# Weight-conversion pieces given fixed places among the expert slots, and the experts' first relu moved to ScalarE and ahead of the w2 splits

## The chip, the cores and the metric

The kernel runs on one core of a Trainium2 chip. A core has five engines with a queue each: PE (TensorE, matmuls), DVE (VectorE), ACT (ScalarE), POOL (GpSimd) and SP (SyncE, which here only issues DMAs). Every engine works through its own queue in the order of the program and waits for the others through semaphores. The metric is the device time of one execution, in microseconds.

## The reference, cut to what matters

```python
def _moe_ref(x, w_gate, w_output_gate, w1, w2):        # x: 1792 x 768, 8 experts, w1: 768 x 1024, w2: 1024 x 768
    e_idx = np.argmax(x @ w_gate, axis=1)
    ...
    for e in range(E):
        mask = e_idx == e
        h = np.maximum(x[mask] @ w1[e], 0.0)
        out[mask] = gate_w[mask, None] * eom[mask, e, None] * (h @ w2[e])

def _moe2_ref(x, w_in, w_out):                         # w_in: 768 x 2048, w_out: 2048 x 768
    h = x @ w_in
    return (h * np.cos(h)) @ w_out

x = sigmoid_attention(q, k, v)                         # 4 x 12 heads, 448 x 64, gives x
return _moe2_ref(_moe_ref(x, ...), w_in, w_out)
```

## The kernel before, in words

The program has three stages: attention, the experts (a mixture-of-experts layer with one expert for each token), and a second dense layer. All large matmuls are done three times, on a high and a low part of both operands, so that every operand is first split: ACT writes the high part (a Copy), DVE subtracts it to get the low part.

**Experts.** Tokens are sorted by expert into slots of 128, each slot with one expert. `slot(s, ...)` does one slot. For the measured data 19 slots, 0 to 18, are active, and new experts begin in slots 4, 6, 10, 11, 14, 15 and 18 (and 0). In a slot PE does, in this order: x times the first half of w1 (six k steps of three matmuls, tile `ph`, named `p` in the trace), three k steps of the second half, four transposes of the first half's relu (`turn_h`, tile `pht`), the other three k steps, six transposes of the next slot's tokens (`turn`, tile `pxt`), the first k step of h times w2 (tile `py`), four transposes of the second half's relu, and the other seven k steps with w2. The relu of each half (`relu`, tiles `hr`) reads PSUM; `turn_h` then has ACT write `hh` and DVE write `hl`.

The weights of an expert come in four quarters of w1 and four of w2, all through the same four buffers `rw`. In the slot before a new expert `split1` splits w1's quarters (`w1h` on ACT, `w1l` on DVE) and then has SP load w2's quarter into the same buffer. In the expert's first slot `split2(i)` splits w2's quarter i (`w2h`, `w2l`) and has SP load a quarter of the w1 that comes after. In other slots both are skipped by a branch on a flag. Before the change, `split2(0)` stands behind the first relu, `split2(1)` behind `turn_h` of the first half, and `split2(2)` and `split2(3)` ahead of `turn_h` of the second half. At the slot's end `scale_y` scales the result (`ysb`).

**Conversion.** The second layer's weights are given in float64, and the chip converts them itself in 48 pieces of 512 columns (`conv`). A piece is, in its first half, ACT's `cta`, POOL's maximum, ACT's `ctu` and DVE's `ctb` and `ctu`; and in its second half four DVE operations (`cta`, `chi`, `ctb`, `clo`). `conv_step()` finishes a piece that is open (`conv_end`), has SP store a finished piece (`conv_store`) and load the raw data of the next one (`conv_load`, two buffers `craw`), and begins a piece; unless told `False` it also finishes it. The attention does 23 pieces, the ends of slots 1 to 17 do one each (`CONV_EARLY = 40`), and the second layer does the other eight, one in each of its units 1 to 8, begun with `conv_step(False)` and finished within the next unit's `product`.

**Second layer.** `units` are pairs of a block of tokens (four blocks of 4, 4, 3 and 3 tiles) and one of 16 chunks of 128 columns. In unit u the program emits: `load_w(u + 5)`, `product(u + 1)` (with `conv_end` inside it, tiles `r`, `gh`, `gl`), `up(u + 2)` on PE, `take(u + 2)` on ACT (tile `p`, which empties PSUM), `angle(u + 2)` on DVE, then from unit 8 to 13 a transpose of the next block's tokens (`turn_y`, tiles `pyt` and `yl`), a conversion piece, `cosine(u + 2)` on ACT and `down(u)` on PE. `up` and `turn_y` share two PSUM buffers in turn. `load_w(c)` may not load a chunk that isn't converted:

```python
ready = max(i for i, (which, h, _) in enumerate(conv_list) if h == (c * P // CW if which == "i" else c // 2))
while conv_at[0] <= ready:
    conv_step()
```

For chunk 12, loaded in unit 7, `ready` is 44; for chunk 14, loaded in unit 9, it is 47.

Of the kernel before, what the change touches and what calls it, by code (L numbers as in the profile page):

```python
# [9 lines left out]
F32 = mybir.dt.float32  # L10
# [12 lines left out]

GATE_STEPS = 7
NEST = 18
CONV_EARLY = 40
PAUSE = "pause"
NRING = 6
ROUTE_AT = [(0, "relu"), (0, 9), (0, 15), (0, 17), (1, 0), (1, 3), (1, "relu"), (1, 9), (1, 14)]
# [25 lines left out]
def tile_attn_moe_cos(ctx: ExitStack, tc: tile.TileContext, q, k, v, wg, wog, w1, w2, w_in, w_out, out):  # L55
# [139 lines left out]
    def conv_end():  # L195
        while conv_rest:
            next(conv_rest.pop(), None)
# [31 lines left out]
            in_offset=bass.IndirectOffsetOnAxis(ap=at, axis=0),  # L229
        )  # L230

    def turn(xg, ps, tag):
        for k0, n_ in ((0, 4), (4, 2)):
            pt = ps.tile([P, 512], F32, tag=tag, name="pxt")
            for kc in range(n_):
                nc.tensor.transpose(pt[:, kc * P : (kc + 1) * P], xg[:, (k0 + kc) * P : (k0 + kc + 1) * P], ident)
            ptv = pt[:, : n_ * P].rearrange("p (k t) -> p k t", t=P)
            nc.scalar.activation(xh[:, k0 : k0 + n_], ptv, AF.Copy)  # L238
            nc.vector.tensor_tensor(
                xl[:, k0 : k0 + n_], ptv, xh[:, k0 : k0 + n_].bitcast(F32), op=ALU.subtract  # L240
            )

    def mm1(ps, nh, kc, first, last):
        i = 2 * nh + kc // 3
# [440 lines left out]
    with ExitStack() as st:  # L685
# [12 lines left out]
        def relu(ps, scalar=False):  # L698
            hr = m2.tile([P, 512], F32, tag="hr", name="hr")
            if scalar:  # L700
                nc.scalar.activation(hr, ps, AF.Relu)
            else:
                nc.vector.tensor_scalar(hr, ps, 0.0, None, op0=ALU.max)
            return hr
# [35 lines left out]
        def slot(s, between, when):  # L740
            nxt = s + 1 < NSLOT
            ahead = min(s, 1)
            hh = m2.tile([P, KF, P], F32R, tag="hh", name="hh", bufs=1)
            hl = m2.tile([P, KF, P], F32R, tag="hl", name="hl", bufs=1)
            with when():
                if 0 < s < NSLOT - 2:
                    gather(xgs[s % 2], idx[:, s + 2 : s + 3])
                if s > 1:
                    new = flag(1, s, SPLIT)
                    ld = flag(3, s, [ENG.SP])  # L750
                    ne = flag(0, s, [ENG.SP], E - 1)

                def split2(i):
                    if s == 0:
                        split(w2r[i], w2h[i], w2l[i])
                    elif s > 1:
                        with tc.If(new != 0):
                            split(w2r[i], w2h[i], w2l[i])
                        with tc.If(ld != 0):
                            nc.sync.dma_start(w1r[i], w1_src_d(ne, i))  # L760

                ph = p0 if s == 0 else ps_h.tile([P, 512], F32, tag="h", name="p0")
                for kc in range(3 if s == 0 else 0, KD):
                    mm1(ph, 0, kc, kc == 0, kc == KD - 1)
                    between(kc)
                hr0 = relu(ph, s == 0)
                between("relu")
                split2(0)
                p1 = ps_h.tile([P, 512], F32, tag="h", name="p1")
                for kc in range(KD):  # L770
                    mm1(p1, 1, kc, kc == 0, kc == KD - 1)
                    if kc == 2:
                        turn_h(hr0, hh, hl, 0)
                        split2(1)
                    between(KD + kc)
                hr1 = relu(p1, s <= 1)
                if 0 < s and nxt:
                    turn(xgs[(s + 1) % 2], ps_t, "t")
                if s > 0:
                    split2(2)  # L780
                    split2(3)
                py = ps_y.tile([P, 2, 512], F32, tag="y", name="py")
                state["py"] = py
                for kc in range(ahead):
                    mm2(py, hh, hl, kc)
                    between(2 * KD + kc)
                turn_h(hr1, hh, hl, 1)
                between("h")
                if s == 0:
                    split2(2)  # L790
                    split2(3)
            if nxt and s >= NSURE:
                split1(s + 1)
            with when():
                for kc in range(ahead, KF):
                    mm2(py, hh, hl, kc)
                    between(2 * KD + kc)
                if s == 0:
                    turn(xgs[1], ps_t, "t")
                elif nxt and s < NSURE:  # L800
                    split1(s + 1)
                if s > 0:
                    scale_y(s)
            if s >= 1 and conv_at[0] < CONV_EARLY:
                conv_step()

        def scale_y(s):
# [208 lines left out]
        split_first(3)  # L1016

        def last_slots(s):
            assert conv_at[0] >= CONV_EARLY
            act = nc.values_load(fl[0:1, 2, s : s + 1], min_val=0, max_val=1)  # L1020
            with tc.If(act != 0):
                slot(s, between(s), nullcontext)
                store_y(s)
                if s + 1 < NSLOT:
                    last_slots(s + 1)
# [254 lines left out]
```

## Time and profile before

| what | value |
|---|---|
| time, median of 3 runs | 1086.42 us (1086.36 to 1087.2) |
| the profiled execution: its time | 1089.18 us |
| the profiled execution: its span | 1087.5 us |
| PE busy | 1038.9 us, 96% of the span |
| DVE busy | 705.1 us, 65% |
| ACT busy | 486.6 us, 45% |
| POOL busy | 168.5 us, 15% |
| mean granted TensorE clock | 0.987 |

The times in the views are from the start of the span, which is shorter than the execution's own time by what lies before the first and after the last instruction. A line such as L703 is a line of the kernel; a wait in square brackets is idle time just before an instruction, and the name behind the arrow is what ended it.

### The profile page before, as it was taken

To read this page: it belongs to the slowest core of one execution; us is meant where nothing else is said; L and a number is where in the kernel's file an instruction comes from. 1 tells how busy PE (TensorE), PEld (TensorE's weight loads), DVE (VectorE), ACT (ScalarE), POOL (GpSimd) and SP (SyncE) were. 2 spreads that over 40 slices of the span, in tenths; PEclk is the share of its full clock that TensorE was granted. 3 is DMA by queue.
4 is the path that set the end of the run, shared out by engine and by line. 5 is a ranking of instruction groups with operands and counts; after the bars stand their busy time and mean duration, and the time that the engine had idled before them with its cause. 6 is when DMAs were issued, how large, how long until landed. Compare 5 with 4: busy or idle time off the path is not lost. (4 is left out here: it accounts for less than half of the span.)

```text
span 1087.5 us, 16874 instructions
## 1 busy us (share of the span) xinstructions
PE 1038.9 (96%) x5836; PEld 832.1 (77%) x5836; DVE 705.1 (65%) x1233; ACT 486.6 (45%) x707; POOL 168.5 (15%) x184
## 2 busy tenths in 40 slices
PE   6999999989999998998997999999999999999997
PEld 3555555568877886886786888788888899999996
DVE  3777778785767458658656599855555555665553
ACT  5777776532445245345334444333333343334332
POOL 3433332011111111211111032003000020001001
PEclk9999999999999999999899999999999999999999
DMA  7899995835578439939835998757644577668741
GB/s 186 250 283 299 261 260 169 306 101 184 182 255 312 125 123 348 322 121 352 269 113 181 392 359 304 259 184 255 244 174 179 184 297 298 247 232 286 261 165 44
DMA packets 118788, 254.68 MB, mean 234 GB/s; under 512 B 9440, under 2 KB 66016, under 8 KB 118688
## 3 DMA queue, kind: packets, MB, share of 16 engines
q1 hardware_dynamic: 114768, 234.19, 63.9%
q0 software_dynamic: 3920, 19.28, 4.6%
q8 instruction: 48, 0.79, 0.3%
q14 instruction: 52, 0.43, 0.1%
HBM read 207.02 MB, written 46.41 MB: 233 GB/s over the span
## 5 line engine op out<-in xcount | busy, mean ns | idle before, releaser
L1172 PE MATMUL o<-wo,gh 128*128 128x512 f32 x448 | 168.4, 397 | 0.0
L155 POOL TENSOR_SCALAR cta<-cta 128x512 f32<-128x512 f32 x48 | 77.3, 1610 | 458.6 <-ACT cta L154 458.6
L1112 PE MATMUL ph<-yh,wi 128*128 128x512 f32 (+1 forms) x318 | 115.3, 363 | 0.0
L1113 PE MATMUL ph<-yl,wi 128*128 128x512 f32 (+1 forms) x318 | 115.2, 362 | 0.0
L1114 PE MATMUL ph<-yh,wi 128*128 128x512 f32 (+1 forms) x318 | 115.2, 362 | 0.0
L1135 ACT ACTIVATE r<-r 128x512 f32<-128x512 f32 (+1 forms) x64 | 37.0, 578 | 168.6 <-DVE r L1130 167.0
L305 ACT ACTIVATE aT<-sc,b_sig 112x896 f32<-112x896 f32 x96 | 91.5, 1005 | 43.2 <-PE sc L302 42.3
L1173 PE MATMUL or<-wo,gh 128*128 128x256 f32 x384 | 108.5, 282 | 0.0
L1172 PEld LDWEIGHTS o<-wo,gh 128*128 128x128 f32 x448 | 84.1, 188 | 17.0
L246 PE MATMUL p<-w1h,xh 128*128 128x512 f32 x228 | 93.3, 409 | 0.3 <-ACT xh L238 0.3
L247 PE MATMUL p<-w1l,xh 128*128 128x512 f32 x228 | 90.7, 398 | 0.0
L248 PE MATMUL p<-w1h,xl 128*128 128x512 f32 x228 | 90.3, 396 | 0.0
L1172 PE MATMUL o<-wo,gl 128*128 128x512 f32 x224 | 88.3, 394 | 0.0
L309 PE MATMUL av<-aT,v 112*64 112x448 f32 x384 | 84.0, 560 | 1.4 <-DVE xT L319 1.4
L1141 DVE TENSOR_TENSOR r<-r,p 128x512 f32<-128x512 f32 (+1 forms) x64 | 40.0, 625 | 66.4 <-ACT r L1136 66.4
L1173 PEld LDWEIGHTS or<-wo,gh 128*128 128x128 f32 x384 | 72.4, 189 | 0.8
L1196 POOL DMA_INDIRECT out_dram<-osb,at x14 | 14.2, 1014 | 368.3 <-DVE osb L1185 277.0
L1126 DVE TENSOR_SCALAR t<-p 128x512 f32<-128x512 f32 (+1 forms) x64 | 27.1, 424 | 66.1 <-ACT p L1121 66.1
L1121 ACT ACTIVATE p<-ph 128x512 f32<-128x512 f32 (+1 forms) x64 | 34.7, 542 | 71.5 <-PE ph L1114 71.5
L1146 DVE TENSOR_TENSOR gl<-r,gh 128x512 fp32r<-128x512 f32 (+1 forms) x64 | 42.5, 664 | 36.4 <-ACT gh L1145 36.4
L1112 PEld LDWEIGHTS ph<-yh,wi 128*128 128x128 f32 x318 | 59.7, 188 | 7.7
L712 ACT ACTIVATE hh<-pht 128x512 fp32r<-128x512 f32 x38 | 22.7, 598 | 94.0 <-PE pht L709 84.2
(255 smaller groups left out, 2438.7 us busy)
## 6 DMA issues: line engine op xcount, KB each, us to landing
rw<-in_moe_w_dram SPq DMA_DIRECT2D x64, 768.0 KB, 6.1
wo<-wo_d SPq DMA_DIRECT2D x64, 768.0 KB, 4.4
wi<-wi_d SPq DMA_DIRECT2D x53, 768.0 KB, 5.9
craw<-in_moe_w_in_dram SPq DMA_DIRECT2D x25, 512.0 KB, 6.4
craw<-in_moe_w_out_dram SPq DMA_DIRECT2D x24, 512.0 KB, 5.5
er<-wi_d SPq DMA_DIRECT2D x11, 768.0 KB, 6.3
ys_d<-ysb SPq DMA_DIRECT2D x19, 384.5 KB, 3.7
wi_d<-chi SPq DMA_DIRECT2D x24, 256.0 KB, 3.1
```

Source lines behind the costliest of these rows:

```text
L155: nc.gpsimd.tensor_scalar(ta.bitcast(F32), ta.bitcast(F32), LEAST, None, op0=ALU.max)
L246: nc.tensor.matmul(ps, xh[:, kc], wh, start=first, stop=False)
L247: nc.tensor.matmul(ps, xh[:, kc], wl, start=False, stop=False)
L248: nc.tensor.matmul(ps, xl[:, kc], wh, start=False, stop=last)
L305: nc.scalar.activation(aT[:, c], ps[:, :, :S], AF.Sigmoid, bias=b_sig[:CP], scale=1.0 / math.sqrt(D))
L309: nc.tensor.matmul(pav[D * j : D * j + D, :S], t["v"][:, j, c, :], aT[:, c, j], start=c == 0, stop=c == NC - 1)
L1112: nc.tensor.matmul(ph[:, :w], wih[:, kc], yh[:, kc, :w], start=kc == 0, stop=False)
L1113: nc.tensor.matmul(ph[:, :w], wih[:, kc], yl[:, kc, :w], start=False, stop=False)
L1114: nc.tensor.matmul(ph[:, :w], wil[:, kc], yh[:, kc, :w], start=False, stop=kc == KD - 1)
L1146: nc.vector.tensor_tensor(gl[:, :w], r, gh[:, :w].bitcast(F32), op=ALU.subtract)
L1172: nc.tensor.matmul(acc[i], g[:, ts_], w[:, :512], start=f, stop=l)
L1173: nc.tensor.matmul(acc["r", i], g[:, ts_], w[:, 512:], start=f and (own or i % 2 == 0), stop=l, skip_group_check=True,)
```

## The change

A table now says where the experts do conversion pieces: `CONV_MID` names slots in which a piece is begun in the middle (behind `split2(3)`) and finished at the slot's end, `CONV_END` those in which a whole piece follows at the end. That makes 15 pieces in place of 17, so the second layer begins at piece 38 and not at 40. The slots 3, 4, 8, 9, 12, 13 and 16 no longer have a piece; slots 1, 2, 6, 7 and 11 have two. The first relu of every slot goes from DVE to ACT. In slots above 0, `split2(1)` moves behind the second relu and ahead of `turn`; `split2(2)` and `split2(3)` move behind `turn_h` of the second half, and the low part of the next slot's tokens (`xl`) is written between these two.

```diff
-CONV_EARLY = 40
+CONV_MID = (1, 2, 6, 7, 11)
+CONV_END = (1, 2, 5, 6, 7, 10, 11, 14, 15, 17)
...
-    def turn(xg, ps, tag):
+    def turn(xg, ps, tag, later=False):
+        low = []
...
-            nc.vector.tensor_tensor(
-                xl[:, k0 : k0 + n_], ptv, xh[:, k0 : k0 + n_].bitcast(F32), op=ALU.subtract
-            )
+            low.append(
+                lambda k=slice(k0, k0 + n_), p=ptv: nc.vector.tensor_tensor(
+                    xl[:, k], p, xh[:, k].bitcast(F32), op=ALU.subtract
+                )
+            )
+            if not later:
+                low.pop()()
+        return low
...
-                hr0 = relu(ph, s == 0)
+                hr0 = relu(ph, True)
                 between("relu")
                 split2(0)
...
                         turn_h(hr0, hh, hl, 0)
-                        split2(1)
+                        if s == 0:
+                            split2(1)
                     between(KD + kc)
                 hr1 = relu(p1, s <= 1)
-                if 0 < s and nxt:
-                    turn(xgs[(s + 1) % 2], ps_t, "t")
+                low = ()
                 if s > 0:
-                    split2(2)
-                    split2(3)
+                    split2(1)
+                    if nxt:
+                        low = turn(xgs[(s + 1) % 2], ps_t, "t", True)
...
                 turn_h(hr1, hh, hl, 1)
                 between("h")
-                if s == 0:
-                    split2(2)
-                    split2(3)
+                split2(2)
+                for f in low:
+                    f()
+                split2(3)
+                if s in CONV_MID:
+                    conv_step(False)
...
-            if s >= 1 and conv_at[0] < CONV_EARLY:
+            conv_end()
+            if s in CONV_END:
                 conv_step()
```

**DVE between slot 3 and slot 4**, where slot 4 begins a new expert. Before, from slot 3's last write (`ysb`) to slot 4's first w2 quarter (`w2l`), with a whole piece (the six rows L157 to L163) and the relu (`hr`) between:

```order
L811 COPY ysb_2624<-idx 128x1
L157 TENSOR_SCALAR ctb<-craw_101 128x512
L158 SCALAR_TENSOR_TENSOR ctu<-ctb,ctu 128x512
L160 TENSOR_SCALAR cta<-cta 128x512
L161 SCALAR_TENSOR_TENSOR chi<-craw_101,cta 128x512
L162 TENSOR_SCALAR ctb<-chi 128x512
L163 TENSOR_TENSOR clo<-ctu,ctb 128x512
L728 TENSOR_LOAD fl
L703 TENSOR_SCALAR hr<-p_3604 128x512
L757 COMPARE_AND_BRANCH
L218 TENSOR_TENSOR w2l_2619<-rw_95,w2h_2615 128x1536
```

Now, from the same write on, as far as the second relu and the second quarter:

```order
L824 COPY ysb_2624<-idx 128x1
L736 TENSOR_LOAD fl
L765 COMPARE_AND_BRANCH
L220 TENSOR_TENSOR w2l_2619<-rw_95,w2h_2615 128x1536
L765 UNCONDITIONAL_BRANCH x2
L767 UNCONDITIONAL_BRANCH
L721 TENSOR_TENSOR hl<-pht,hh 128x512
L711 TENSOR_SCALAR hr<-p_3646 128x512
L765 COMPARE_AND_BRANCH
L220 TENSOR_TENSOR w2l_2620<-rw_96,w2h_2616 128x1536
```

The piece and the first relu have left this place, and the second quarter now stands behind the second relu. Before the new experts of slots 6, 11, 15 and 18 the piece is still there, since 5, 10, 14 and 17 are in `CONV_END`; only the relu has left.

**ACT between slot 6 and slot 7.** Before, from slot 6's `ysb` through slot 7's first rows:

```order
L809 ACTIVATE ysb_2624<-py,scs 128x512
L154 ACTIVATE cta<-craw_100 128x512
L156 ACTIVATE ctu<-craw_100 128x512
L728 TENSOR_LOAD fl
L728 ISA x2
L757 COMPARE_AND_BRANCH
L217 ACTIVATE w2h_2615<-rw_95 128x1536
L757 UNCONDITIONAL_BRANCH x2
L759 UNCONDITIONAL_BRANCH
L712 ACTIVATE hh<-pht 128x512
```

Now:

```order
L822 ACTIVATE ysb_2624<-py,scs 128x512
L156 ACTIVATE cta<-craw_101 128x512
L158 ACTIVATE ctu<-craw_101 128x512
L736 TENSOR_LOAD fl
L736 ISA x2
L709 ACTIVATE hr<-p_4307 128x512
L765 COMPARE_AND_BRANCH
L219 ACTIVATE w2h_2615<-rw_95 128x1536
L765 UNCONDITIONAL_BRANCH x2
L767 UNCONDITIONAL_BRANCH
L720 ACTIVATE hh<-pht 128x512
```

The relu now stands on ACT behind the piece's two operations. Their raw data, `craw_101`, is loaded by the `conv_step(False)` in the middle of slot 6, whose DMAs stand on SP behind slot 6's four loads of w1 and behind two stores; before, it was loaded at the end of slot 5. The same holds at the ends of slots 11, 1, 2 and 7, where slots 1, 2 and 7 have no loads of w1 in `split2` ahead of it, and slot 1 has those that the routing issues.

**DVE in unit 7 of the second layer**, around `product(8)` (`r<-r,p` and `gl`). Before, from the last operation of the angle on:

```order
L1130 SCALAR_TENSOR_TENSOR r<-t,r 128x512
L157 TENSOR_SCALAR ctb<-craw_101 128x512
L158 SCALAR_TENSOR_TENSOR ctu<-ctb,ctu 128x512
L1141 TENSOR_TENSOR r<-r,p 128x512
L160 TENSOR_SCALAR cta<-cta 128x512
L161 SCALAR_TENSOR_TENSOR chi<-craw_101,cta 128x512
L162 TENSOR_SCALAR ctb<-chi 128x512
L163 TENSOR_TENSOR clo<-ctu,ctb 128x512
L1146 TENSOR_TENSOR gl<-r,gh 128x512
```

Now, from the second half of unit 6's piece on:

```order
L162 TENSOR_SCALAR cta<-cta 128x512
L163 SCALAR_TENSOR_TENSOR chi<-craw_101,cta 128x512
L164 TENSOR_SCALAR ctb<-chi 128x512
L165 TENSOR_TENSOR clo<-ctu,ctb 128x512
L159 TENSOR_SCALAR ctb<-craw_100 128x512
L160 SCALAR_TENSOR_TENSOR ctu<-ctb,ctu 128x512
L162 TENSOR_SCALAR cta<-cta 128x512
L163 SCALAR_TENSOR_TENSOR chi<-craw_100,cta 128x512
L164 TENSOR_SCALAR ctb<-chi 128x512
L165 TENSOR_TENSOR clo<-ctu,ctb 128x512
L1154 TENSOR_TENSOR r<-r,p 128x512
L1159 TENSOR_TENSOR gl<-r,gh 128x512
```

A whole piece (44) has come in ahead of `product(8)`, because `load_w(12)` needs it and the unit begins at piece 44 and not at 46. In the same way piece 47 now comes in whole ahead of `product(10)` in unit 9, behind the second half of piece 46. Units 1 to 6 have one piece each, as before.

## Rows read from the trace of the kernel before

**Rows 1.** Experts by stretch: length, busy PE PEld DVE ACT POOL, clock, DMA share, GB/s.

```profile
255.10:591.70 336.60, 318.11 (x1668) 265.69 (x1666) 222.01 (x294) 143.47 (x175) 51.10 (x38) 0.98 0.66 226
273.32:291.49 18.17, 18.17 (x100) 15.46 (x99) 12.61 (x17) 9.47 (x11) 2.82 (x2) 1.00 0.42 139
291.49:311.76 20.27, 18.80 (x100) 15.39 (x99) 15.63 (x20) 9.27 (x11) 2.60 (x2) 1.00 1.01 354
330.30:350.18 19.88, 18.78 (x101) 15.40 (x99) 15.54 (x20) 9.28 (x11) 2.61 (x2) 1.00 1.00 356
405.09:425.67 20.58, 18.78 (x100) 15.40 (x99) 18.16 (x22) 12.48 (x14) 2.61 (x2) 1.00 1.00 354
425.67:449.97 24.30, 19.95 (x101) 16.55 (x100) 18.55 (x21) 12.02 (x13) 2.95 (x2) 0.93 0.98 337
486.44:506.98 20.54, 18.87 (x101) 15.44 (x99) 18.18 (x22) 12.47 (x14) 2.61 (x2) 1.00 0.99 357
506.98:533.83 26.85, 21.24 (x101) 17.57 (x100) 18.73 (x21) 11.91 (x13) 2.95 (x2) 0.87 0.90 306
570.89:591.70 20.81, 18.98 (x100) 15.29 (x98) 15.89 (x20) 9.28 (x11) 2.82 (x2) 1.00 0.61 216
```

**Rows 2.** PE in order of time: start, duration, instruction, wait; slots 3, 4, 15.

```profile
279.50 0.66 PE L709 MATMUL pht<-ident,hr 128*128 128x128 f32 x4
...
284.12 0.48 PE L722 MATMUL py<-w2h,hh 128*128 128x512 f32 x1
...
298.21 0.66 PE L709 MATMUL pht<-ident,hr 128*128 128x128 f32 x4 [0.41 <-DVE hr L703]
...
518.04 1.12 PE L709 MATMUL pht<-ident,hr 128*128 128x128 f32 x4 [4.76 <-DVE hr L703]
```

**Rows 3.** Groups by line: count, busy us, mean ns, idle time before and its releasers.

```profile
L218 DVE TENSOR_TENSOR w2l<-rw,w2h 128x1536 fp32r<-128x1536 f32 x32 | 55.4, 1753 | 5.0 <-ACT w2h L217 5.0
L217 ACT ACTIVATE w2h<-rw 128x1536 fp32r<-128x1536 f32 x32 | 46.6, 1484 | 0.3 <-DMA rw<-in_moe_w_dram 0.3
...
L703 DVE TENSOR_SCALAR hr<-p 128x512 f32<-128x512 f32 x35 | 24.1, 690 | 11.2 <-PE p L248 7.5 <-issue 3.0 <-DVE clo L163 0.5
...
L701 ACT ACTIVATE hr<-p 128x512 f32<-128x512 f32 x3 | 1.8, 598 | 7.7 <-PE p L248 7.6
```

**Rows 4.** DVE in order of time, a piece in slot 3, slot 15's relu.

```profile
274.70 0.42 DVE L157 TENSOR_SCALAR ctb<-craw 128x512 uint32<-128x512 uint32 x1
...
278.15 0.69 DVE L163 TENSOR_TENSOR clo<-ctu,ctb 128x512 fp32r<-128x512 f32 x1
...
517.30 0.69 DVE L703 TENSOR_SCALAR hr<-p 128x512 f32<-128x512 f32 x1 [1.08 <-issue]
```

**Rows 5.** DMA issues from 336 to 350 us: KB, median us to landing.

```profile
craw<-in_moe_w_in_dram SPq DMA_DIRECT2D x1, 512.0 KB, 9.1
```

**Rows 6.** DMA issues from 346 to 356 us.

```profile
craw<-in_moe_w_in_dram SPq DMA_DIRECT2D x1, 512.0 KB, 5.3
```

**Rows 7.** DVE in order of time, pieces in the second layer.

```profile
655.76 0.42 DVE L157 TENSOR_SCALAR ctb<-craw 128x512 uint32<-128x512 uint32 x1
...
664.44 0.42 DVE L157 TENSOR_SCALAR ctb<-craw 128x512 uint32<-128x512 uint32 x1
...
691.42 0.42 DVE L157 TENSOR_SCALAR ctb<-craw 128x512 uint32<-128x512 uint32 x1
...
694.20 0.69 DVE L163 TENSOR_TENSOR clo<-ctu,ctb 128x512 fp32r<-128x512 f32 x1
```

**Rows 8.** PE in order of time, second layer.

```profile
655.89 0.40 PE L1172 MATMUL o<-wo,gh 128*128 128x512 f32 x1
...
664.21 0.40 PE L1172 MATMUL o<-wo,gh 128*128 128x512 f32 x1
...
691.57 0.33 PE L1097 MATMUL pyt<-ident,yg_r 128*128 128x128 f32 x1 [1.81 <-DVE yl L1101]
...
696.70 0.50 PE L1112 MATMUL ph<-yh,er 128*128 128x512 f32 x1 [0.27 <-ACT p L1121]
```

More of the change, by code (lines that the diff above doesn't have):

```diff
@@ L1018, in last_slots @@
         def last_slots(s):
-            assert conv_at[0] >= CONV_EARLY
+            assert s > max(CONV_END)
             act = nc.values_load(fl[0:1, 2, s : s + 1], min_val=0, max_val=1)
```

## The prediction, made before the changed kernel ran

> **What bounds the kernel now.** I read the page first: PE is busy for 1038.9 of 1087.5 us, so the time is PE's work plus the places where PE waits or runs at its lower clock. Then PE's waits, which lie nearly all in the experts and at one point of the second layer; so I cut the experts by slots and then read the two stretches in order of time. An undisturbed slot (slot 3) takes 18.17 us [rows 1]. The 17 slots 2 to 18 take 336.60 us, and 17 x 18.17 is 308.9: 27.7 us are lost. By the same rows slots 4, 6, 10 and 14, the first of a new expert, lose 2.10, 1.71, 2.41 and 2.37 (8.6 together), slots 11 and 15, where a new expert follows a one-slot expert, 6.13 and 8.68, slot 18 2.64, and the ten others 1.7 in all. What PE waits for is the relu on DVE: 0.41 us in slot 4, 4.76 us in slot 15 [rows 2], because the splits of w1, a conversion piece and a branch stand ahead of it. After the long waits the granted clock falls: its mean is 0.93 in slot 11 and 0.87 in slot 15, where PE is busy for 19.95 and 21.24 us with work that takes 18.8 us in slots 4 and 10 [rows 1], so 1.2 and 2.4 of the loss are matmuls at 1.2 instead of 2.4 GHz.
>
> In the second layer PE should be the bound, and in units 1 to 8, which carry a piece each, it is not quite. DVE's period there is 664.44 - 655.76 = 8.68 us [rows 7], PE's is 664.21 - 655.89 = 8.32 us [rows 8]. DVE falls behind by 0.36 us per unit, and at 691.57 PE has used up its lead: it waits 1.81 us for DVE's `yl`, then 0.27 us for ACT's `p`, which follows DVE's `product(10)` [rows 8]. From there on any further DVE work ahead of these two goes onto PE one for one.
>
> **The change part by part.**
>
> *The relu on ACT.* ACT takes 0.598 us where DVE takes 0.690 [rows 3], and PE needs the result 6.18 us after the slot's start (279.50 - 273.32) [rows 1, 2]; the product is done after 4.1 us (18 of the 27 equal matmuls until then). So there are 1.5 us of cover beyond the relu's own time, and the sum has nothing for it. The Trainium skill, "ScalarE: Activation LUTs", section "Rules for kernel authors", speaks against the change: it sends relu to VectorE and not to ScalarE, with VectorE up to about three times as fast in bf16. By that the sum would be some 5 us higher, as an estimate. The trace differs for this tile, float32 out of PSUM: 598 against 690 ns [rows 3].
>
> *First slots of an expert, 4, 6, 10, 14.* I lay the new order out with 1.48 us for `w2h` and 1.75 for `w2l` [rows 3], 0.6 to 0.7 for the small operations, from the slot's start: relu until 4.9; quarter 0 on ACT 6.3, on DVE 8.1; `hl` 8.8; second relu 9.5; quarter 1 on DVE 11.2; second transposes on PE 10.4, `hh` 11.5; quarter 2 on ACT 12.9, on DVE 14.7. PE's last seven k steps take 291.49 - 284.12 = 7.37 us, 1.05 each [rows 1, 2], so PE needs quarter 2's low part at 14.3. It comes 0.4 to 0.6 late. `xl` (1.0) and quarter 3 follow until 17.3 on DVE; needed at 16.8: 0.5 late. So 1.1 us stay lost in each: 8.6 becomes 4.4, a gain of 4.2. That slot 6 still has a piece ahead doesn't matter: DVE is through with it before `w2h` lets the first quarter start. The w1 loads issued behind quarters 2 and 3 go out about 1 us later; the 1 MB of stores and raw data that no longer competes at the ends of slots 9 and 13 pays for that, where DMA share is 1.00 and 0.99 [rows 1]. POOL loses work and nothing there waits on it.
>
> *Slot 18*: no `xl` between the quarters, so some 0.2 us stay: gain 2.4.
>
> *Slots 11 and 15.* The piece is still ahead of DVE's first quarter, as is in slot 15 a gap of 1.08 us that no wait explains [rows 4]. But PE now passes the first transposes (the relu comes from ACT, behind the piece's two operations there, 0.7 late) and does 4 us of work before it needs `w2l`, which comes 2.0 and 2.7 us late; later quarters add 1.2. With part of the clock loss I leave 4.2 and 4.9 us lost: gains 1.9 and 3.8.
>
> *The other slots* lose their relu waits: gain 1.5 of the 1.7. Sum of gains 4.2 + 2.4 + 1.9 + 3.8 + 1.5 = **13.8 us**.
>
> *The new wait.* At the ends of slots 6 and 11 the raw data is issued on SP behind the last w1 load (quarter 3, after 17.3 us; after 20.4 in slot 11), and two stores: about 19 us after slot 6's start, which is where slot 7 begins. A raw load takes 5.3 us on quiet queues [rows 6] and 9.1 on full ones [rows 5]. ACT's queue stands in order: `cta`, `ctu`, then the relu, 1.9 us together, and PE waits on it at 6.15. Data later than 4.3 us in the slot therefore stalls PE one for one. Landing 5.3 to 9.1 us after the slot's start costs 1.0 to 4.8 us per slot; I take 1.9, nearer the lower end, since the w1 loads are ending by then. In slot 2 the raw data follows the routing's four w1 loads, which were issued earlier in slot 1 than these: I take half, 0.9 (0 to 2). Together **4.7 us** (2 to 11.6).
>
> *The second layer.* Pieces 44 and 47 stand whole in DVE's way, ahead of `product(8)` and `product(10)`. A piece without waits takes from 691.42 to 694.81 (694.20 + 0.69, less the overlap with its successor), 3.4 us [rows 7]; one that waits for ACT and POOL from 274.70 to 278.76 (278.15 + 0.69, less the same overlap), 4.06 us [rows 4]. These wait in part, since `cta` and `ctu` can begin only when the piece before has left their buffers: 3.85 each, 7.7 together (6.8 to 8.1). PE has no lead left, so `up(12)` starts 7.7 us later. No later unit gives it back, because PE is the bound there. The last of these waits is some 4.3 us long; a wait of 4.76 us lowered the clock for 2.4 us of cost [rows 1, 2], so 1.6 more (0 to 2.6): **9.3 us**.
>
> *Sum*: -13.8 + 4.7 + 9.3 = +0.2. On the profiled execution's 1089.18 us that is 1089.4; it stands 2.76 us above the median, so the forecast is **1086.6 us**, no change. Differences under 0.2%, 2.2 us, are what a measurement of this kernel can't tell from none.
>
> **The rivals.**
>
> *Faster: the raw data comes in time.* If it lands within 4.3 us of the slot's start the 4.7 us vanish: 1081.9. For it: the quarters may run earlier than I laid them out, and so may the issue. Against it: the issue has to come 5 us earlier, and no raw load in these rows lands in under 5.3 us.
>
> *Slower: the raw data lands as on full queues.* At 9.1 us behind issue, slots 7 and 12 lose 4.8 each and slot 2 some 2: 11.6 in place of 4.7, so 1093.5; each 2.2 us beyond the sum decides, which is landing 1.0 us later in both slots. For it: DMA share is 1.00 in slot 6 and 0.98 in slot 11, where w1 loads are ahead [rows 1]. The Trainium skill, "Trainium Kernel Development and Optimization", section "Key Constraints", says that DMAs of all queues share the same 16 engines and interleave, so the raw load would share with the w1 loads ahead of it and not pass them; the 5.3 and 9.1 us agree.
>
> *The relu is late on ACT.* If its operation behind the slot's others took 0.3 us more than the cover in each of 17 slots, 5 us would be lost: 1091.7. Against it: 598 ns, and the 1.5 us [rows 1 to 3].
>
> *The second layer takes the pieces for nothing.* If DVE had slack in units 7 to 9 the 9.3 us would go: 1077.3. Against it stand the two waits of PE for DVE and ACT at just that point [rows 8].
>
> **How the numbers follow.** No change 0.40, raw data in time 0.22, second layer for nothing 0.06, raw data late 0.29, relu late 0.03. Faster is the second and third: 0.28; same 0.40; slower the fourth and fifth: 0.32. The range leaves out the outer tenth on both sides: 1081 takes in the raw data in time with the lower bound of a piece, 1092 most of the late case. The likeliest case's own range is 1084.4 to 1088.8.
>
> **What would show it.** Right: slots 4, 10, 14 at about 19.2 us, with PE's waits at L722 for `w2l` and none for the relu; slots 7 and 12 at about 20 us, ACT waiting for `craw` just ahead of `cta`; in the second layer a wait of PE of 4 us for ACT's `p` at `up(12)`, and some 8 to 10 us more for units 7 to 9. Wrong: slot 7 at 18.2 us, or no wait of PE between units 8 and 10, or slots 11 and 15 as long as before because the w1 or w2 quarters land later.

## The result, and the profile after

The changed kernel takes 1095.94 us against 1086.81 us before, measured beside it: a ratio of 1.0087 with a 95% interval of 1.0069 to 1.0105. It is slower by 0.87%, where I had forecast no change (1086.6 us) and a range that ended at 1092. One run of 3,582 us is left out of the ratio as disturbed.

The profiled spans, 1092.6 and 1087.5 us, are only 5.1 apart, because the attention, which the change leaves alone, took 3.14 us longer in the trace of before: PE's first matmul on w1 stands at 207.79 us there and at 204.65 after. So both traces are counted from that matmul on, and cut at the second layer's first matmul. First the view by stretches of before (columns as in [rows 1]):

```profile
207.79:601.24 393.45, 366.29 (x1945) 304.90 (x1943) 261.04 (x400) 161.59 (x203) 54.03 (x41) 0.98 0.63 213
601.24:1087.50 486.26, 476.04 (x2558) 421.33 (x2556) 295.79 (x545) 178.55 (x308) 42.34 (x46) 0.99 0.66 242
```

The same two stretches after, and seven slots:

```profile
252.55:275.53 22.98, 19.91 (x100) 16.67 (x99) 10.66 (x19) 5.81 (x10) 4.18 (x3) 0.93 0.68 225
...
293.66:312.94 19.28, 18.65 (x100) 15.53 (x99) 13.10 (x13) 8.89 (x11) 2.29 (x1) 1.00 0.95 313
...
350.58:371.41 20.83, 18.35 (x100) 15.39 (x99) 10.56 (x19) 5.80 (x10) 4.19 (x3) 1.00 0.74 237
...
426.93:450.28 23.35, 20.98 (x100) 16.55 (x99) 19.35 (x22) 13.76 (x16) 4.44 (x3) 0.93 0.99 349
450.28:471.19 20.91, 18.47 (x101) 15.39 (x100) 9.06 (x17) 4.46 (x8) 7.43 (x7) 1.00 0.82 271
471.19:489.31 18.12, 18.12 (x100) 15.52 (x99) 7.33 (x10) 8.57 (x10) 0.94 (x1) 1.00 0.16 52
...
508.59:532.78 24.19, 20.86 (x100) 16.68 (x99) 18.33 (x20) 12.63 (x14) 2.95 (x2) 0.93 0.97 337
...
204.65:597.75 393.10, 367.91 (x1944) 306.05 (x1943) 244.31 (x370) 171.31 (x217) 54.26 (x39) 0.98 0.62 208
597.75:1092.60 494.85, 479.04 (x2559) 422.86 (x2557) 302.63 (x557) 181.42 (x312) 45.07 (x48) 0.99 0.66 243
```

The experts as a whole gained 0.35 us and the second layer lost 8.59: +8.24, which is the difference of the medians but for 0.9. Behind the 0.35 stand two sums that cancel. By slots (each from its first matmul on w1 to the next slot's, slot 18 to its last on w2; E1 to E8 are experiments told below):

| slot | before | after | E1 | E2 | E3 | E4 | E8 |
|---|---|---|---|---|---|---|---|
| 2 | 18.22 | 22.98 | 23.12 | 18.11 | 18.12 | 18.11 | 18.21 |
| 4 | 20.27 | 19.28 | 19.29 | 19.29 | 19.65 | 19.29 | 21.09 |
| 6 | 19.88 | 19.51 | 19.29 | 19.96 | 19.64 | 19.28 | 21.15 |
| 7 | 18.34 | 20.83 | 23.01 | 18.12 | 18.11 | 18.12 | 18.29 |
| 10 | 20.58 | 19.28 | 19.28 | 19.29 | 19.65 | 19.27 | 21.10 |
| 11 | 24.30 | 23.35 | 24.20 | 24.78 | 25.15 | 24.36 | 25.88 |
| 12 | 18.28 | 20.91 | 20.35 | 18.12 | 18.12 | 18.13 | 18.38 |
| 14 | 20.54 | 19.28 | 19.28 | 19.27 | 19.70 | 19.90 | 21.46 |
| 15 | 26.85 | 24.19 | 24.20 | 23.93 | 25.64 | 24.27 | 26.91 |
| 18 | 20.78 | 19.71 | 19.95 | 19.73 | 19.95 | 19.58 | 23.79 |
| all experts | 393.45 | 393.10 | 395.47 | 384.17 | 386.96 | 383.72 | 402.15 |
| second layer | 486.26 | 494.85 | 485.77 | 495.26 | 486.36 | 486.38 | 486.04 |

Slots 2, 7 and 12 lost 4.76, 2.49 and 2.63 us, 9.88 together, and slot 1 0.82 (in the experiments it takes 19.62 to 21.20 whatever its pieces, so that these 0.82 are not told from scatter); all else gained 11.05.

**What PE waits for in slots 2, 7 and 12.** PE after, in order of time (compare slot 15 in [rows 2]):

```profile
261.93 0.66 PE L717 MATMUL pht<-ident,hr 128*128 128x128 f32 x4 [3.07 <-ACTq L765]
...
359.39 0.66 PE L717 MATMUL pht<-ident,hr 128*128 128x128 f32 x4 [2.48 <-ACTq L765]
...
459.05 0.66 PE L717 MATMUL pht<-ident,hr 128*128 128x128 f32 x4 [2.44 <-ACTq L765]
```

The row names a branch of ACT's queue just behind the relu. ACT itself, after, slots 2, 7 and 12:

```profile
259.90 0.67 ACT L156 ACTIVATE cta<-craw 128x512 f32<-128x512 f32 x1 [6.46 <-DMA craw<-in_moe_w_in_dram]
260.46 0.65 ACT L158 ACTIVATE ctu<-craw 128x512 f32<-128x512 uint32 x1
261.28 0.60 ACT L709 ACTIVATE hr<-p 128x512 f32<-128x512 f32 x1 [0.17 <-ACT ctu L158]
...
357.52 0.68 ACT L156 ACTIVATE cta<-craw 128x512 f32<-128x512 f32 x1 [6.05 <-DMA craw<-in_moe_w_in_dram]
358.10 0.64 ACT L158 ACTIVATE ctu<-craw 128x512 f32<-128x512 uint32 x1
358.74 0.60 ACT L709 ACTIVATE hr<-p 128x512 f32<-128x512 f32 x1
...
457.30 0.67 ACT L156 ACTIVATE cta<-craw 128x512 f32<-128x512 f32 x1 [6.13 <-DMA craw<-in_moe_w_out_dram]
```

ACT sits six microseconds in front of a piece's first operation until its raw data lands, and the relu, whose input is long there, stands behind it. SP's queue shows when that data was asked for (start, duration, DMA; the last two rows are slot 6's):

```profile
245.59 2.25 SPq L1000 DMA_DIRECT2D rw<-in_moe_w_dram  x4
250.82 0.37 SPq L179 DMA_DIRECT2D wo_d<-chi  x1
252.86 0.36 SPq L179 DMA_DIRECT2D wo_d<-clo  x1
255.28 0.36 SPq L139 DMA_DIRECT2D craw<-in_moe_w_in_dram  x1
...
342.27 6.91 SPq L768 DMA_DIRECT2D rw<-in_moe_w_dram  x4
...
350.48 0.73 SPq L139 DMA_DIRECT2D craw<-in_moe_w_in_dram  x1
```

In slot 6 the issue comes at 350.48, slot 7 begins at 350.58, and the load takes 7.04 us, between the 5.3 and 9.1 of [rows 5, 6]. In slot 1 it is another thing: the load takes only 4.6 us, but SP comes to it 2.73 us after slot 2 has begun. What SP waited for there, 225 to 275 us (us in total, times, longest):

```profile
SPq L179 <- DMA rw<-in_moe_w_dram: 4.5, 2, 2.9
SPq L139 <- DMA rw<-in_moe_w_dram: 1.6, 1, 1.6
```

The stores and the raw load are on other data than `rw`, and yet SP holds them back until loads of w1 ahead have landed, 6.1 us in all. The semaphore numbers in the trace's records say why. The two stores and the raw load each wait for the semaphore on which their own landing will be counted (107, 108 and 100), and the first three of the four w1 loads are still counting on these same three. SP's trace of after has 437 issues whose semaphore an earlier DMA had used, and none goes out before that DMA has landed. So what holds SP here is the program's reuse of a few completion semaphores, and not the data.

**The second layer.** PE's waits of units 6 to 10 (compare [rows 8]):

```profile
678.39 0.33 PE L1110 MATMUL pyt<-ident,yg_r 128*128 128x128 f32 x1 [1.31 <-ACT p L1134]
...
685.19 0.50 PE L1125 MATMUL ph<-yh,wi 128*128 128x512 f32 x1 [1.93 <-ACT p L1134]
...
691.54 0.33 PE L1110 MATMUL pyt<-ident,yg_r 128*128 128x128 f32 x1 [0.35 <-DVE yl L1114]
...
700.46 0.79 PE L1125 MATMUL ph<-yh,er 128*128 128x512 f32 x1 [4.06 <-ACT p L1134]
```

DVE there, the first operation of the forced pieces 44 and 47 and the product behind each (compare [rows 7]):

```profile
672.82 0.71 DVE L159 TENSOR_SCALAR ctb<-craw 128x512 uint32<-128x512 uint32 x1
...
676.50 0.68 DVE L1154 TENSOR_TENSOR r<-r,p 128x512 f32<-128x512 f32 x1
...
694.90 0.72 DVE L159 TENSOR_SCALAR ctb<-craw 128x512 uint32<-128x512 uint32 x1
...
698.58 0.68 DVE L1154 TENSOR_TENSOR r<-r,p 128x512 f32<-128x512 f32 x1
```

And two stretches there by engine, columns as above:

```profile
684.00:692.00 8.00, 6.46 (x23) 4.93 (x23) 7.66 (x17) 4.22 (x7) 1.79 (x1) 0.79 0.99 365
...
700.00:704.00 4.00, 3.54 (x9) 2.85 (x10) 3.86 (x7) 1.24 (x3) 0.00 (x0) 0.57 0.98 321
```

The waits add up to 7.65 us against 2.08 before, so 5.57 more. PE's busy time rose by 479.04 - 476.04 = 3.00, the same matmuls at a granted clock of 0.79 and 0.57. Together 8.57: the second layer's loss is accounted for.

### The profile page after: what moved, and what is told of

Read it like the earlier page. It is cut to its first block, busy times and chain, and to the rows that moved or that the text cites. A ratio compares the mean times of both kernels' runs of the same rounds, so it can differ in the third digit from the quotient of the medians.

```text
span 1092.6 us, 17168 instructions
## 1 busy us (share of the span) xinstructions
PE 1043.1 (95%) x5836; PEld 835.2 (76%) x5836; DVE 693.9 (64%) x1215; ACT 499.2 (46%) x725; POOL 171.6 (16%) x184
## 3 DMA queue, kind: packets, MB, share of 16 engines
q0 software_dynamic: 3920, 19.28, 5.0%
## 5 line engine op out<-in xcount | busy, mean ns | idle before, releaser
L157 POOL TENSOR_SCALAR cta<-cta 128x512 f32<-128x512 f32 x48 | 80.4, 1676 | 408.9 <-ACT cta L156 408.9
L730 PE MATMUL py<-w2l,hh 128*128 128x512 f32 x152 | 61.6, 405 | 8.7 <-DVE w2l L220 8.0
L220 DVE TENSOR_TENSOR w2l<-rw,w2h 128x1536 fp32r<-128x1536 f32 x32 | 56.0, 1752 | 16.1 <-ACT w2h L219 12.5
```

The source lines that it names most:

```text
L157: nc.gpsimd.tensor_scalar(ta.bitcast(F32), ta.bitcast(F32), LEAST, None, op0=ALU.max)
L730: nc.tensor.matmul(py[:, 0, :], ht[:, kc], wt[:, :512], start=f, stop=l)
```

## The experiments

Theory 1 was that the change is two losses and a gain that have nothing to do with each other: late raw data (9.9 us), forced pieces (8.6 us), and a gain from the relu and the order of the quarters (11 us) to which the new places of the pieces add nothing. All ratios are against the kernel before, on the same chip.

| run | ratio | 95% interval | median us |
|---|---|---|---|
| E1: changed, 40 pieces | 1.0023 | 1.0009 to 1.0037 | 1087.64 |
| E2: changed, raw data early | 0.9997 | 0.9985 to 1.0009 | 1085.44 |
| E3: before, relu alone | 0.9942 | 0.9927 to 0.9958 | 1079.02 |
| E4: before, relu and order | 0.9912 | 0.9898 to 0.9926 | 1075.9 |
| E5: E1 and E2 | 0.9909 | 0.9888 to 0.993 | 1075.91 |
| E6: E4, 45 pieces | 0.9888 | 0.9867 to 0.991 | 1072.43 |
| E7: E4, 39 pieces | 0.9964 | 0.9952 to 0.9976 | 1080.71 |
| E8: before, order alone | 1.009 | 1.0068 to 1.0112 | 1095.06 |
| E9: E8, second quarter alone | 1.0021 | 1.0005 to 1.0036 | 1086.37 |
| E10: E6 without two pieces | 0.9876 | 0.9855 to 0.9897 | 1072.69 |

**E1: the second layer's two pieces back.**

```diff
-CONV_END = (1, 2, 5, 6, 7, 10, 11, 14, 15, 17)
+CONV_END = (1, 2, 5, 6, 7, 10, 11, 12, 14, 15, 16, 17)
```

> The changed kernel with two more pieces in the slots (whole ones at the ends of slots 12 and 16), so that the second layer begins at piece 40 as before. Against 1086.8 us before and 1095.9 after. Theory 1: the second layer alone costs 8.6 us (495.1 of before's kind against 486.3), because pieces 44 and 47 stand whole ahead of two products; without them it falls back, and the slots stay as they are after the change: 1087.3 us (1086 to 1089), no wait of 4 us for p in the second layer, slots 2, 7 and 12 still 20.8 to 23 us. Rival: the second layer is longer for another reason (the weights stored later, the phase of PE's two buffers): at least 1093 us.

1.0023 against 1.0087, the second layer 485.77 us, its waits 1.8 and 0.3 as before, slots 2, 7 and 12 still 20.35 to 23.12: theory 1. (Slot 7 here takes 2.18 us more than after: the raw load takes 7.5 us there and not 7.0, PE waits 3.06 us and not 2.48, and the slot's granted clock is 0.93 and not 1.00.)

**E2: the raw data early.**

```diff
+                if s > 1 and s in CONV_MID:
+                    conv_store()
+                    conv_load(conv_at[0] + 1)
...
                 hr0 = relu(ph, True)
+                if s == 1:
+                    conv_store()
+                    conv_load(conv_at[0] + 1)
...
-                    conv_step(False)
+                    conv_step(False, True)
```

The second argument leaves the store and the load out of the step in the middle.

> The changed kernel with the raw data of the end pieces of slots 2, 6, 7 and 11 issued at the slot's start and of slot 1 behind its first relu, so ahead of the w1 loads on SP; nothing else moved, still 38 pieces in the slots. Theory 1: the data of slots 1, 6 and 11 is late because SP issues it late (behind the w1 loads): slots 2, 7 and 12 fall to 18.2 us each, the waits of PE for the relu there (3.07, 2.48, 2.44 us) go, slot 1 stays within 0.5: 10 us less, 1086 us (1084.5 to 1088). Rival 1: the 16 DMA engines are shared, so that the raw data only changes places with w1 and w2 quarters, which come later by as much: over 1092 us. Rival 2: the second piece in a slot is itself too much for ACT and DVE ahead of the relu: 1095 us, slots 2, 7, 12 as long as after.

Slots 2, 7 and 12 of E2:

```profile
252.13:270.24 18.11, 18.11 (x100) 15.54 (x99) 10.85 (x19) 5.95 (x10) 4.51 (x3) 1.00 0.69 222
...
345.74:363.86 18.12, 18.12 (x100) 15.53 (x99) 10.88 (x19) 5.93 (x10) 4.52 (x3) 1.00 0.81 268
...
444.16:462.28 18.12, 18.12 (x100) 15.53 (x99) 9.37 (x17) 4.72 (x8) 7.76 (x7) 1.00 0.82 289
```

All three are free of waits with the same pieces, so the lateness came from the place on SP's queue and not from the second piece's work. Slots 6 and 11, where the raw data now goes ahead of w1 loads, are 0.45 and 1.43 longer than after; slot 11 ranges from 22.80 to 24.78 over the changed kernel, E1, E2 and E4 to E7, so the rival's share can't be told from that.

**E3 and E4: relu alone, and relu with the order, with the old places.**

```diff
-                hr0 = relu(ph, s == 0)
+                hr0 = relu(ph, True)
```

> The kernel before with the first relu on ScalarE in every slot and nothing else. Theory 1: the relu's waits (14.2 us in the kernel before) go, but in the slots of new experts most of the time comes back as waits for the low parts of w2, since the piece still stands ahead of the first quarter and the later quarters are in their old order: 1082 us (1079 to 1085). Rival 1: the relu's wait was the whole of it: 1073 us or less. Rival 2: the relu is late on ScalarE behind the piece's two operations: 1086 us or more.

E4 is the changed kernel with these two lines:

```diff
-CONV_MID = (1, 2, 6, 7, 11)
-CONV_END = (1, 2, 5, 6, 7, 10, 11, 14, 15, 17)
+CONV_MID = ()
+CONV_END = tuple(range(1, 18))
```

> The changed kernel with the pieces as before (a whole one at the end of each of slots 1 to 17, none in the middle, 40 before the second layer), so relu and the new order of the quarters alone. Theory 1: gains come from relu and order, and the places of the pieces gave only the two losses: slots 4, 6, 10, 14 at about 19.5 us, 11 and 15 as after (23.4 and 24.2), slots 2, 7, 12 at 18.2, second layer as before: about 10 us less than before, 1077 us (1075 to 1080). Rival: a piece ahead of a new expert's first quarter is what costs, so that with the old places slots 4, 10, 14 stay at 20.3 to 20.6 us: 1081 us or more.

Slots 4, 11, 14 and 15 of E4:

```profile
289.02:308.31 19.29, 18.66 (x101) 15.53 (x100) 16.14 (x19) 10.01 (x13) 3.72 (x2) 1.00 0.98 346
...
419.32:443.68 24.36, 20.87 (x101) 16.59 (x99) 20.12 (x21) 14.10 (x15) 2.95 (x2) 0.93 0.99 344
...
479.92:499.82 19.90, 19.33 (x100) 15.47 (x99) 17.69 (x20) 12.56 (x15) 3.73 (x2) 1.00 1.00 359
499.82:524.09 24.27, 20.75 (x101) 16.56 (x100) 18.74 (x21) 13.09 (x15) 2.94 (x2) 0.93 0.98 339
```

Both times lie within theory 1's ranges. The relu alone takes 6.49 us off the experts, relu and order 9.73. Slots 4 and 10 are 19.29 and 19.27 long with a piece ahead of the first quarter and 19.28 without one (after): once the relu is on ACT, the piece is hidden there. Only slot 14, 0.62 longer, owes something to it: of the runs with relu and order it takes 19.27 to 19.29 in the four without a piece at slot 13's end (after, E1, E2, E5), and 19.48 to 19.90 in E4, E6 and E7, which have one.

**E5: both losses cured at once.** E2's edit, and E1's line:

```diff
-CONV_END = (1, 2, 5, 6, 7, 10, 11, 14, 15, 17)
+CONV_END = (1, 2, 5, 6, 7, 10, 11, 12, 14, 15, 16, 17)
```

> Both cures at once on the changed kernel: its own places for pieces and two more at the ends of slots 12 and 16 (40 before the second layer), and the raw data of the end pieces of slots 1, 2, 6, 7, 11 issued ahead of the w1 loads. Theory 1: the two losses are separate and add up, so both go: 0.9997 and 1.0023 of before against 1.0087 give 0.9934 of before, 1079 us (1077 to 1080.5). And the places themselves bring nothing: not faster than relu and order with the old places (0.9912 of before). Rival: the places do help at the new experts once the losses are gone: 0.989 of before or less.

0.9909, not told apart from E4's 0.9912: with both losses cured nothing is left that the change lost, and the new places bring nothing that these intervals can show. The 0.9934 of the sum lies just outside the interval. E1's slot 7, 2.18 us longer than after, is 0.0020 of the time and makes up most of the gap.

**E6: more pieces in slots that have room.** E2's edit with other places.

```diff
-CONV_MID = (1, 2, 6, 7, 11)
-CONV_END = (1, 2, 5, 6, 7, 10, 11, 14, 15, 17)
+CONV_MID = (1, 2, 7, 8, 12)
+CONV_END = tuple(range(1, 18))
```

> Relu and order of the change, a whole piece at the end of each of slots 1 to 17 as before, and five more in the middle of slots 1, 2, 7, 8 and 12, whose slots issue no w1 loads in split2, with the raw data of the end piece issued early: 45 pieces before the second layer, three left for it. Theory 1: DVE's work sets the second layer's pace while it carries a piece per unit, so with three left the wait of PE for yl and p at unit 9 (2.1 us before) goes: 0.9912 less 0.002 of before, 1073.5 us (1072 to 1075), slots 2, 7, 8, 12 still 18.1. Rival: the pieces in the slots cost what they save: 1075.9 us or more.

E6's second layer, by engine:

```profile
586.52:1070.20 483.68, 475.55 (x2558) 421.11 (x2556) 277.11 (x515) 172.71 (x298) 33.31 (x41) 0.99 0.62 232
```

It is 2.70 us shorter than E4's 486.38, and its view of PE's waits is empty; slots 2, 7, 8 and 12 are 18.10 to 18.13. The ratios of E4 and E6 alone don't tell the two apart, since their intervals overlap.

**E7: one forced piece in place of two.**

```diff
-CONV_END = tuple(range(1, 18))
+CONV_END = tuple(range(1, 17))
```

> Relu and order of the change, whole pieces at the ends of slots 1 to 16 and none elsewhere, so the second layer begins at piece 39: only piece 47 is forced whole (ahead of product(10)), 44 not. Theory 1: each forced piece costs its own time on DVE, half of the 8.6 us: 4.3 us over the 1075.9 of relu and order with 40 pieces, 0.995 of before, 1080 us (1079 to 1081.5). Rival 1: the first forced piece only uses up slack and the second pays: 1076.5 us or less. Rival 2: one is enough to upset the unit's rhythm: 1083 us or more.

PE in E7's second layer:

```profile
675.80 0.33 PE L1110 MATMUL pyt<-ident,yg_r 128*128 128x128 f32 x1 [1.20 <-DVE yl L1114]
684.83 0.50 PE L1125 MATMUL ph<-yh,er 128*128 128x512 f32 x1 [4.17 <-ACT p L1134]
```

The second layer takes 490.58 us, 4.20 over E4: half of 8.6, with the 4 us wait left and the two of 1.31 and 1.93 gone. The ratio rose by 0.0052, which is 5.6 us where 4.3 was expected; E7's profiled execution is the fastest of its twelve, so the trace may show less of the loss than the median.

**E8 and E9: the order without the relu.** E8 is E4 with this line:

```diff
-                hr0 = relu(ph, True)
+                hr0 = relu(ph, s == 0)
```

> The order of the quarters alone: pieces as before, the first relu on VectorE as before, w2's second quarter behind the second relu, third and fourth behind the second transposes. Theory 1: the order takes away the waits for the later quarters, but the relu's waits stay (up to 4.8 us in slots 11 and 15): 0.2 to 0.5% less than before, 1082 us (1080 to 1085); the order is worth as much here as on top of the relu (3 us). Rival: without the early relu the order does nothing, since the relu's wait comes first and the quarters are done by then: within 0.15% of before.

Both expectations missed: the order alone costs 0.9%, and E3 and E8 don't add up to E4. E8's PE, DVE and ACT at the passage from slot 3 to slot 4, which begins at 288.45:

```profile
296.34 0.66 PE L717 MATMUL pht<-ident,hr 128*128 128x128 f32 x4 [1.57 <-DVE hr L711]
...
284.57 6.76 DVE L220 TENSOR_TENSOR w1l<-rw,w1h 128x1536 fp32r<-128x1536 f32 x4 [0.72 <-ACT w1h L219]
...
282.86 5.62 ACT L219 ACTIVATE w1h<-rw 128x1536 fp32r<-128x1536 f32 x4 [0.90 <-DVEq L765]
```

The splits of w1 now begin 3.88 us ahead of slot 4 (5.00 before), because the skipped third and fourth quarter now stand between slot 3's second `hh` and `w1h` in ACT's queue. The view puts ACT's 0.90 us down to DVE's branch, but by the trace's records ACT's queue comes to that check at 282.78, when DVE's signal of 282.75 is already there. From `hh`'s end at 281.96 on, ACT's queue is at work itself: two skipped blocks, in which it first checks that `hh` has ended, then a load of the flag and another branch. The relu on DVE, behind these splits, is later by as much: 1.57 against 0.41 us of waiting [rows 2]. E9 puts those two quarters and `xl` back:

```diff
                     if nxt:
-                        low = turn(xgs[(s + 1) % 2], ps_t, "t", True)
+                        low = turn(xgs[(s + 1) % 2], ps_t, "t")
+                    split2(2)
+                    split2(3)
...
-                split2(2)
-                for f in low:
-                    f()
-                split2(3)
+                if s == 0:
+                    split2(2)
+                    split2(3)
```

> The first relu on VectorE and the pieces as before; of the new order only that w2's second quarter stands behind the second relu; the low part of the next tokens, third and fourth quarter are where they were before (ahead of the second transposes). Order with all three moved and relu on VectorE gave 1.009 of before. Theory 1: that loss comes from the third and fourth quarter standing behind the second transposes, also where their branch is skipped, which makes ACT's w1h and DVE's w1l begin 3.9 instead of 5.0 us before the end of the slot ahead of a new expert and so the relu on VectorE 1.1 us later: with them back, slot 4 waits 0.4 us for the relu again and the time is within 0.3% of before. Rival: the second quarter behind the second relu is what costs: 1.006 of before or more.

1.0021, and in slot 4 (E9, same two engines):

```profile
295.89 0.66 PE L717 MATMUL pht<-ident,hr 128*128 128x128 f32 x4 [0.56 <-DVE hr L711]
...
282.50 5.62 ACT L219 ACTIVATE w1h<-rw 128x1536 fp32r<-128x1536 f32 x4
```

ACT's wait is gone (`w1h` starts as `hh` ends, at 282.52) and PE's is 0.56. Over the first slots of the seven experts that follow the first, PE's waits for the first relu add up to 10.65 us before, 19.61 in E8 and 10.27 in E9, and E8's experts are 8.70 us longer than before: the loss of the order alone is the relu on DVE, held up by later splits. That skipped blocks do it was read in slot 4 alone; ahead of slots 11 and 15 the quarters aren't skipped but split. With the relu on ACT it no longer stands behind DVE's splits.

**E10: slots 11 and 15 without the piece ahead of them.**

```diff
-CONV_END = tuple(range(1, 18))
+CONV_END = (1, 2, 3, 4, 5, 6, 7, 8, 9, 11, 12, 13, 15, 16, 17)
```

> As the fastest version so far (relu and order of the change, whole pieces at the ends of slots 1 to 17, five more in the middle of 1, 2, 7, 8, 12, 0.9888 of before) but without the pieces at the ends of slots 10 and 14, so that none stands ahead of the first w2 quarter of the one-slot experts' successors in slots 11 and 15; 43 before the second layer. Theory 1: slots 11 and 15 are held by the loads of w1 and w2 (DMA share near 1.0 there), not by the piece: they stay at 22.8 to 25 us, the time within 0.2% of 0.9888 (1070.5 to 1075 us). Rival: the piece holds DVE and ACT up there, and each of the two slots falls by 1.5 us or more: 0.9862 of before or less.

Neither: against E6 slots 11 and 15 fell from 23.29 and 24.95 to 22.60 and 22.55, 3.1 us, but slots 10 and 14 rose from 19.32 and 19.48 to 20.54 and 20.65, 2.4 us, with PE now waiting for w1's own parts at the border between the slots (1.10 and 1.30 us at slot 11's beginning). The ratio's interval takes in E6. The loss moved more than it shrank. PE's waits for the first `w2l`, 1.71 and 2.37 us in E6, are gone, so the piece did hold DVE up there. The waits at the border are for loads: around slot 11's beginning each of ACT's four `w1h` starts 0.10 to 0.24 us after its load has landed, in E10 as in E6. Why the first of these loads took 9.8 us in E10 and 7.9 in E6 stays open.

## Why the prediction was wrong

**The step that failed is "The new wait"**, sized at 4.7 us (0.9 for slot 2, 1.9 each for 7 and 12) and measured at 9.88 (4.76, 2.49, 2.63), near its upper bound of 11.6. The sum said +0.2 and the two stretches show +8.24; of the 8.0 between, this step is 5.2, the gain that was too large 2.8 and slot 1, which the sum left out, 0.8, while the second layer takes 0.7 off. In slots 7 and 12 the mechanism was as described, and E2 shows it. The threshold was right to 0.1 us: data that lands later than 4.3 us in the slot stalls PE one for one. It landed at 6.94 in slot 7 and 7.02 in slot 12, which by that gives 2.64 and 2.72; the slots are 2.71 and 2.79 over 18.12. The issue too came where I had put it, 19.41 us after slot 6's start. What I had wrong was the flight: I had the data land 6.2 us after the slot's start, "nearer the lower end", and the load took 7.0 us. [Rows 6], my lower end, aren't quiet queues as I said: the DMA share from that load's issue to its landing is 0.96. What differs is how much SP had issued ahead that had not landed yet: 897 KB in three stores there (5.3 us), 2,048 KB in two w1 loads and two stores in slots 6 and 11 (7.0 and 7.1 us), 2,433 KB in two loads and three stores in [rows 5] (9.1 us); slot 1's 1,280 KB (4.6 us) don't fit that order, and no run tests it.

Worse was slot 2. I halved its price because the w1 loads there are issued earlier, as if only a shared DMA engine could make the raw data late; but SP's own queue stood still until those loads had landed, because the DMAs behind them use the same semaphores, so that the issue came 2.73 us into slot 2. PE waited 3.07 us, and then ran at a mean clock of 0.93, busy 19.91 us where 18.1 is usual: 1.8 more that I had not counted at all.

The rival "as on full queues" gave 1093.5 us and is the nearest to the result, but not by its own reason: no load into these three slots took 9.1 us. The Trainium skill, "Trainium Kernel Development and Optimization", section "Key Constraints", says that DMAs of all queues share the engines and interleave. The 7.0 us of slot 7 agree with that; slot 2's 4.6 us don't need it.

**The gain** was 13.8 by the sum and 11.05 measured, of which 0.8 lie in slot 0 and behind slot 18, where the sum had nothing. Slots 4, 10 and 14 came out at 19.28, forecast 19.2, with the two waits of a quarter that I had laid out (0.38 and 0.25 us). Slot 18 gained 1.07 and not 2.4: the same two waits, which I had put down in part to `xl`, are there without it. Slots 11 and 15 gained 0.95 and 2.66, not 1.9 and 3.8. ACT, DVE and PE in slot 15, after, which begins at 508.59:

```profile
511.71 1.49 ACT L219 ACTIVATE w1h<-rw 128x1536 fp32r<-128x1536 f32 x1 [0.53 <-DMA rw<-in_moe_w_dram]
...
515.29 1.48 ACT L219 ACTIVATE w2h<-rw 128x1536 fp32r<-128x1536 f32 x1
...
520.22 1.76 DVE L220 TENSOR_TENSOR w2l<-rw,w2h 128x1536 fp32r<-128x1536 f32 x1 [1.33 <-DMA rw<-in_moe_w_dram]
...
522.03 0.51 PE L730 MATMUL py<-w2l,hh 128*128 128x512 f32 x1 [2.86 <-DVE w2l L220]
```

The first `w2l` starts 11.63 us after the slot's start, 10.92 before. The 1.33 us ahead of it are not a wait for its load, though the view says so: ACT began to split the same data at 515.29. DVE's queue reads flags and branches there, as it does in the 1.08 us of before [rows 4]. What came later is all of DVE's work ahead of it, because w1's last quarter landed 2.94 us into the slot (1.89 before): I had set the later issue of the w1 loads against the stores that no longer compete, and put it at nothing. Behind that split stands the piece, and E10 shows that without it PE doesn't wait for the first `w2l`.

**The relu on ACT at no cost** was right; in slots 11 and 15, where I had it 0.7 us late, PE waits 0.39 and 0.31 us for it. Groups by line after (compare [rows 3]):

```profile
L709 ACT ACTIVATE hr<-p 128x512 f32<-128x512 f32 x21 | 12.5, 596 | 39.8 <-PE p L256 38.7 <-ACT ctu L158 0.9
...
L711 DVE TENSOR_SCALAR hr<-p 128x512 f32<-128x512 f32 x17 | 11.7, 687 | 5.7 <-PE p L256 5.3
```

596 ns against 687, and E3 gains 0.58% with that one edit. The rule of the Trainium skill ("ScalarE: Activation LUTs", "Rules for kernel authors") that sends relu to VectorE doesn't hold for this tile of float32 out of PSUM, the less so where VectorE's queue is the late one. The 5 us that the prediction made of that rule don't follow from it: as an estimate, even at three times VectorE's 0.690 us the relu would take 2.07 us, and its own time on ACT with its cover is 2.1.

**The second layer** was sized at 9.3 and measured at 8.59; E1 takes it away and E7 halves it. A forced piece takes 3.68 us, not 3.85. Its make-up differed: 5.57 of waits and 3.00 of lowered clock, where I had 7.7 and 1.6, so that the total is near by luck: the two errors offset each other. The last wait, 4.06 us, was forecast at 4.3, at the same instruction.

**What I did not ask** was what each part of the gain depends on. I credited the new places of the pieces with part of the gain in slots 4, 10 and 14; E4 shows that relu and order give it with the old places, so the places had their two costs and, but for some tenths in slot 14, no gain.

## What to carry to other kernels

When a transfer is moved, read the queue that issues it: what stands ahead of it there, and what that itself waits for, may cost more than the transfer's own time. A wait that lowers the clock is paid for again in slower matmuls, here 3.07 us of waiting with 1.8 us more. Check a releaser that the profile names against the other engines' rows: the 1.33 us of slot 15 and E8's 0.90 us had other causes than the names behind them. When a change has several parts, ask of each what it still gains once the others are made; here the relu had already hidden what the pieces were moved away for. The best kernel of the study (E6, 0.9888; by the intervals E4, E5 and E10 are not told apart from it) keeps the old places, adds pieces only in slots that neither begin nor end an expert, and asks for their data early in the slot.

## What the runs showed that I had not expected

- Skipped blocks cost time on the engine that skips them: in E8 ACT stood idle for 0.90 us between `hh` and `w1h`, where its queue passed two quarters that it didn't split, loaded a flag and branched.
- SP held two stores and a load back for 6.1 us until loads of other data, which had the same semaphores, had landed.
- Waits of 2.44 and 2.48 us left the granted clock of their slots at 1.00; one of 3.07 us brought it to 0.93, as one of 3.06 did in E1's slot 7; in slot 11 two of 0.39 and 1.91 us, in a stretch with gaps between the matmuls as well, also to 0.93.
- Slot 11 took from 22.80 to 24.78 us in the single executions of the changed kernel, E1, E2 and E4 to E7, which all have the same work for its quarters on ACT and DVE.
